# Issuing the head of a gate/up pass inside the stage before it, in a two-layer linear-attention and gated-MLP kernel

## The chip, the cores and the metric

One Trainium2 chip, one of its cores. The metric is the device time of one execution in microseconds (us), the median of several runs. Engines: PE (matmul), DVE (VectorE), ACT (ScalarE), POOL (GpSimd), SP (issues the DMAs).

## The reference

The input x has 2048 tokens of width D = 1024 in bfloat16. Block A and block B are applied twice, with the same weights both times:

```
def _A_ref(x, wqkv, wo):                 # 32 heads of 32
    q, k, v = split(x @ wqkv)
    phi = lambda t: jnp.where(t > 0, t + 1, jnp.exp(t)) + 1e-6
    pq, pk = phi(q), phi(k)
    kv, z = einsum("bhsd,bhse->bhde", pk, v), einsum("bhsd->bhd", pk)
    o = einsum("bhqd,bhde->bhqe", pq, kv) / (einsum("bhqd,bhd->bhq", pq, z)[..., None] + 1e-6)
    return merge_heads(o) @ wo
def _B_ref(x, w_gate, w_up, w_down):     # F = 3584
    return ((x @ w_gate) * (x @ w_up)) @ w_down

x = x + _A_ref(_layernorm(x), wqkv, wo)
x = x + _B_ref(_layernorm(x), w_gate, w_up, w_down)
(the same two lines again)
```

## The kernel before

Every operation goes through one recorder, `P.add(engine, fn, reads, writes)`: an engine runs its operations in the order in which they are recorded, and waits are put in where a region of SBUF, a PSUM bank or a DMA demands one. So the order of the Python calls is the order of each engine's queue, and a waiting instruction holds all that stand behind it on its engine. DMAs are all issued by SP, in recorded order too. An instruction's line in the profile is that of the helper that records it (L662 is any DVE tensor_tensor of the helper `tt`, L665 any scalar_tensor_tensor of `stt`, L404 any plain DMA).

Tokens are handled in 16 tiles of 128. A layer is one `layer_A` and one `layer_B`.

`layer_A`: projections of k and q (L767), then 16 matrix chunks (L851), each with a small product `kvt` (L863) whose last result of each half DVE masks (L868). Beside the chunks `norm(i)` prepares the queries of one tile: DVE multiply (L787), reduce (L790), add (L792), reciprocal (L794), POOL multiply (L796), and a transposing DMA. `NNORM` = 14 of the 16 run there. Then come four held-back q projections, among them `wprod` (L891), matmuls whose results DVE (L898) and ACT (L896) evacuate. Last is the **y loop**, over the 16 tiles: two matmul groups of eight for each tile (`y_grp`, L939), the first added to the residual by DVE (L945), the second seeded (L933) and evacuated (L947) by ACT, in four banks in turn. Beside it the layer norm for block B (class `LN`) goes through a pipeline of one step per tile: statistics on DVE (`start`, L430), a scale (`b1_one`, L441), the normalised row by ACT (`b2_one`, L447) into one of two row buffers `O_XN`, and a transposing DMA from it (`step_t`, L518).

`layer_B`: two passes over 1024 tokens each. A pass is `gateup` (14 pairs of weight columns, Strassen-Winograd products of 512-column matmuls, L1016) and `down` (seven products "1 2 7 4 6 5 3", each four tiles of two groups of seven matmuls, L1285). Weights come through a ring of five slots (`ring_issue`). The order of the steps in a pair is written out by hand in `ORDERS[(second layer, pass)]`: `P` is a product, `D` its last product and `M` the evacuation, `T` a tick that runs other DVE work, `R` a ring load, `S1`/`S5` the weight sums of one pair, and a mark `+` or `'` takes the step of the pair after or before. `L2SETS` names products that are split a second time, into seven groups of two 256-column matmuls (L1082): `11`, `16`, `17` are the steps of product 1, with results handed on in between by ACT (`seed`, L1097; L1107; L1125) and DVE (`join`, L1100). Layer 1 pass 0 splits none and makes its weight combinations itself (`prep_s`); layer 1 pass 1 splits products 1 and 5 and makes the weight sums on DVE; layer 2 splits 1, 5, 3, 2 in both passes and loads the sums (`sp_load`) from what layer 1 stored. The combinations of the activations (`x_ops`, in the list `XQ`) are popped one by one: in the y loop, in products 6 and 5 of `down(0)`, and at the latest where a step needs them (`x_need`).

The first steps of a pass have nothing between them: the pass starts with the steps marked `+` alone, since no other pair is under way.

Of the kernel before, what the change touches and what calls it, by code (L numbers as in the profile page):

```python
# [180 lines left out]
def build_kernel(nc, A_x, A_wqkv, A_wo, B_w_gate, B_w_up, B_w_down, out):  # L181
# [52 lines left out]
    O_ZACC = O_WQ + SZ_W  # L234
    O_GT = O_ZACC + 4096
    RB = take(NST * D * 2)
    O_XR = RB
# [54 lines left out]
    KTA = [dkey("ta%d" % i) for i in range(2)]  # L292
    KTL = [dkey("tl%d" % i) for i in range(2)]
    KTF = [dkey("tf%d" % i) for i in range(NST)]
# [11 lines left out]
    with ExitStack() as es:  # L306
# [62 lines left out]
        B_Z = [5, 6]  # L369
        B_YY = [5, 6, 7, 3]  # L370
        B_GX = [0, 1]
        B_GY = [2, 3]
# [81 lines left out]
        class LN:  # L454
# [12 lines left out]
            def dst(self, n):  # L467
                if self.to == "A0":
                    return xr[:, n, :], r_xr(n)
                return xn[n % 2], R(O_XN[n % 2], D * 2)  # L470

# [42 lines left out]
            def transpose(self, n):  # L514
                d, r = self.dst(n)
                i = self.order[n]
                if self.use_dma:
                    P.add("sp", lambda e: e.dma_start_transpose(xnT[:, :, i * 128:(i + 1) * 128], d),  # L518
                          rd=r, wr=r_xT(i * 128, (i + 1) * 128), dma_sem=KTF[i] if self.to == "A0" else KTL[n % 2])
# [82 lines left out]
        def stash(i):  # L602
            dma(xscr[i * 128:(i + 1) * 128, :], x_res[:, i, :], R(V_X + i * 32, 32), KXS[i], rd=r_x(i))

        def sp_place(ps_, p, g):
            xp = O_X + (8 * ps_ + 3) * D * 2
            o = {"12": (xp, RC), "53": (xp + 4096, O_R + 12288)}[g][p % 2]
            return o, R(V_SP + 64 * p + 32 * SPG.index(g), 32)
# [16 lines left out]
        def sp_load(ps_, p, g):  # L625
            if (first_b[0], ps_, p, g) in sp_done:
                return
            sp_done.add((first_b[0], ps_, p, g))
            o, rv = sp_place(ps_, p, g)
            dma(vh(o, 2048), spscr[2 * p + SPG.index(g)], R(o, 4096), KSP[g, p % 2], rd=rv)  # L630

# [125 lines left out]

        def layer_A(lnp, nxt, first):
            kq_i = [0]
# [141 lines left out]
            for n in range(2 * KT):  # L901
# [24 lines left out]
            for g in range(4, 8):  # L926
                wprod(NG + g, [0, 2, 1, 3][g - 4], g % 2 == 0)
            proj_q(*held[3])()

            def y_seed(n):  # L930
                if n < NST:
                    xs, bank = x_res[:, tok[n], 512:1024], B_YY[(2 * n + 1) % 4]
                    P.add("act", lambda e: e.copy(psb(bank), xs), rd=r_x(tok[n], 512, 1024), pwr=[bank])  # L933

            def y_grp(i, dh, n):
                bank = B_YY[(2 * n + dh) % 4]

# [17 lines left out]
            for i in range(NST):  # L955
                if na[0] < NST:
                    if i % 3 == 2:
                        norm(tok[na[0]])
                        na[0] += 1
                elif RG["n"] < NR:  # L960
                    ring_issue()
                nxt.step_t(1)
                nxt.b1_one()
                if i >= 2 and (first or i < 14):
                    nxt.start(i - 2)
                y_grp(tok[i], 0, i)
                y_seed(i + 1)
                nxt.b2_one()
                y_grp(tok[i], 1, i)
                if not first and i == 12:  # L970
                    for k in range(5):
                        stash(3 + k)
                if not first and i == 14:
                    first_b[0] = False
                    for g in SPG:
                        sp_load(0, 0, g)
                if nxt.t_next >= 8 and not RG["tq"]:
                    RG["tq"] = True
                    XQ.extend(x_ops(0, L2SETS[not first, 0]))
                x_pop(2 if i > 11 else 1)  # L980
            nxt.use_dma = False
            nxt.on_act = False

        def layer_B(lnp, nxt, first):
            is_last = nxt is None
            lnp.use_dma = True
            lnp.on_act = False
            lnp.need(7)
            if not RG["tq"]:
                XQ.extend(x_ops(0, L2SETS[not first, 0]))  # L990
            if not is_last:
                nxt.use_dma = True
                nxt.on_act = False

            def pair(ps_, p, l2):
# [159 lines left out]
                def sums(g, mode):  # L1155
# [17 lines left out]
                    tt(sp[:, 3], wA[:, :, 1], sp[:, 1], ALU.subtract, rp[1] + rA, rp[3])  # L1173
                    dma(spscr[2 * p + SPG.index(g)], vh(o, 2048), rv, KSPW[g, p % 2], rd=R(o, 4096))

# [13 lines left out]
            def gateup(ps_, ticks, l2):  # L1189
# [7 lines left out]
                def emit(it, tk):  # L1197
# [10 lines left out]
                    if p == 0:  # L1208
                        x_need(tk)
                        x_pop()  # L1210
                    if tk[0] == "P":
# [19 lines left out]

                if jit:
                    prep_s(n0)
                    prep_s(n0 + 1)
                for it in range(-1, NP):
                    for tk in order:
                        emit(it, tk)

                def tail():
# [9 lines left out]
                return tail  # L1249

            def down(ps_, ticks, tail):
                i0 = ps_ * 8
# [18 lines left out]
                for qi, q in enumerate(DPROD):  # L1271
# [75 lines left out]
            def dticks0(q, t):  # L1347
# [39 lines left out]

            if first:
                wd_tick(0)
            if first:  # L1390
                for k in range(5):
                    stash(3 + k)
            tail = gateup(0, ticks0, L2SETS[not first, 0])
            if first:
                wd_tick(2 * NJ)
            lnp.need(NST - 1)
            XQ.extend(x_ops(1, L2SETS[not first, 1]))
            down(0, dticks0, tail)
            tail = gateup(1, ticks1, L2SETS[not first, 1])
            down(1, dticks1, tail)  # L1400
            lnp.use_dma = False
            lnp.on_act = False
        dh0 = D // 2
# [16 lines left out]
        alt = [4, 5, 6, 7, 0, 1, 2, 3, 12, 13, 14, 15, 8, 9, 10, 11]  # L1420
        lnA = LN("A0", nat)
        lnB = LN("B", nat)
        layer_A(lnA, lnB, True)
        lnA = LN("A", alt)
        layer_B(lnB, lnA, True)
        lnB = LN("B", alt)
        layer_A(lnA, lnB, False)
        layer_B(lnB, None, False)

# [37 lines left out]
```

## Time and profile before

| | us |
|---|---|
| median of 3 runs | 1486.23 |
| lowest, highest | 1483.78, 1487.76 |
| the profiled execution, its own time | 1487.03 |
| its span, first to last instruction | 1485.3 |
| PE busy | 1459.4 |
| DVE busy | 1089.3 |
| ACT busy | 572.7 |
| POOL busy | 216.1 |
| mean granted PE clock | 0.999 |

All times below are from the start of the span. A busy matmul is longer than the step from one to the next, since they are pipelined: the time lost before a late group is counted from where the group would have started.

### The profile page before, as it was taken

How to read it: one execution, taken by the hardware profiler on the slowest of the kernel's cores; microseconds unless marked ns; L12 is line 12 of the kernel's file. 1: busy time of each engine (PE TensorE's matmuls, PEld its weight loads, DVE VectorE, ACT ScalarE, POOL GpSimd, SP SyncE). 2: the span in 40 equal slices, each digit the busy share in tenths (PEclk: the TensorE clock that was granted, in tenths of full speed). 3: DMA queues.
4: the chain of work that ended last, by engine and by line, in shares of the span. 5: the costliest groups of instructions: out<-in, count | busy, mean ns of one | idle time of the engine just before them, and what ended most of it. 6: DMA issues, size and time to landing. Idle time of an engine off the chain costs nothing.

```text
span 1485.3 us, 20620 instructions
## 1 busy us (share of the span) xinstructions
PE 1459.4 (98%) x7830; PEld 749.3 (50%) x7830; DVE 1089.3 (73%) x1990; ACT 572.7 (39%) x1179; POOL 216.1 (15%) x239
## 2 busy tenths in 40 slices
PE   8999989999999999999999999999999999999999
PEld 3434434444444455554444444446666445666544
DVE  7976777877766599875569769879877575777753
ACT  3332246333310155550013322477776004777400
POOL 4542632000000000000024337210000000000000
PEclk9999999999999999999999999999999999999999
DMA  8799746988885789975364437677965766777642
GB/s 269 131 171 235 160 120 156 272 262 262 261 286 184 231 260 293 295 261 204 124 213 109 132 94 149 178 180 253 283 265 199 237 210 227 261 265 253 210 172 97
DMA packets 268338, 312.78 MB, mean 211 GB/s; under 512 B 161616, under 2 KB 214608, under 8 KB 268240
## 3 DMA queue, kind: packets, MB, share of 16 engines
q1 hardware_dynamic: 268240, 311.48, 69.5%
q8 instruction: 61, 1.00, 0.3%
q14 instruction: 37, 0.30, 0.1%
HBM read 233.31 MB, written 69.21 MB: 204 GB/s over the span
## 4 chain that ended last, share of the span: by engine, by line
PE 88%; DMA 5%; DVE 5%; issue 1%; ACT 1%; POOL 1%; SPq 0%; DVEq 0%; ACTq 0%; POOLq 0%
PE ps L1016 29%; PE ps L1285 23%; PE ps L1082 14%; PE ps L767 12%; PE ps L851 5%; DMA arena<-arena 4%; PE ps L939 4%; DVE arena L787 1%; DVE arena L790 1%; DVE arena L430 1%; DMA arena<-in_A_wqkv_dram 1%; DMA arena<-sp_scratch 1%; DVE arena L662 0%; POOL arena L796 0%; PE ps L891 0%
## 5 line engine op out<-in xcount | busy, mean ns | idle before, releaser
L665 DVE SCALAR_TENSOR_TENSOR arena<-ps,arena 128x512 f16<-128x512 f32 (+2 forms) x508 | 340.5, 686 | 204.0 <-PE ps L1285 150.4
L1016 PE MATMUL ps<-arena 128*128 128x512 f16 x2016 | 478.7, 379 | 1.0 <-DVE arena L662 1.0
L662 DVE TENSOR_TENSOR arena<-arena 128x512 f16<-128x512 f16 (+4 forms) x624 | 309.3, 520 | 60.3 <-ACT arena L1125 48.8
L1285 PE MATMUL ps<-arena 128*128 128x512 f16 (+1 forms) x1568 | 339.4, 379 | 0.0
L1016 PEld LDWEIGHTS ps<-arena 128*128 128x128 f16 (+1 forms) x2016 | 192.1, 98 | 188.3 <-ACT arena L1021 13.6
L1082 PE MATMUL ps<-arena 128*128 128x256 f16 x1960 | 259.4, 273 | 6.6 <-DVE ps L1100 2.4
L1285 PEld LDWEIGHTS ps<-arena 128*128 128x128 f16 x1568 | 153.4, 98 | 185.0
L1082 PEld LDWEIGHTS ps<-arena 128*128 128x128 f16 (+1 forms) x1960 | 189.1, 98 | 90.7 <-DVE ps L1100 11.1
L767 PE MATMUL ps<-arena 128*128 128x512 bf16 x1024 | 225.4, 380 | 8.0 <-DMA arena<-arena 4.6
L1021 ACT ACTIVATE arena<-ps 128x512 f16<-128x512 f32 x224 | 133.7, 597 | 114.9 <-PE ps L1016 113.0
L576 ACT ACTIVATE arena<-ps 128x512 f32<-128x512 f32 x128 | 76.3, 597 | 243.7 <-PE ps L767 221.7
L767 PEld LDWEIGHTS ps<-arena 128*128 128x128 f16 x1024 | 99.3, 98 | 129.3 <-DMA arena<-arena 8.2
L1097 ACT COPY ps<-ps 128x256 f32<-128x256 f32 x168 | 61.8, 369 | 212.5 <-PE ps L1082 210.0
L851 PE MATMUL ps<-arena 128*128 128x512 bf16 x512 | 115.4, 379 | 0.0
L433 POOL TENSOR_SCALAR arena<-arena 128x1 f32<-128x1 f32 x64 | 21.0, 327 | 629.5 <-DVE arena L432 629.5
L939 PE MATMUL ps<-arena 128*128 128x512 bf16 x512 | 111.0, 379 | 1.1 <-ACT ps L933 1.1
L1046 ACT COPY ps<-ps 128x512 f32<-128x512 f32 x112 | 64.2, 573 | 87.7 <-PE ps L1016 52.1
L430 DVE BATCH_NORM_STATS2 arena<-arena 128x6 f32<-128x512 bf16 x128 | 88.1, 688 | 10.7 <-DMA arena<-in_A_x_dram 6.2
L796 POOL TENSOR_TENSOR arena<-arena 128x1024 f16<-128x1024 f32 x32 | 78.2, 2444 | 97.9 <-DVE arena L794 81.1
L577 DVE TENSOR_SCALAR arena<-arena 128x512 f32<-128x512 f32 x128 | 65.8, 514 | 35.6 <-ACT arena L576 34.5
L579 DVE SCALAR_TENSOR_TENSOR arena<-ps,arena 128x512 bf16<-128x512 f32 x128 | 88.5, 691 | 4.4
L1100 DVE TENSOR_TENSOR ps<-ps,arena 128x256 f32<-128x256 f32 x168 | 69.3, 427 | 27.3 <-PE ps L1082 13.7
(51 smaller groups left out, 712.7 us busy)
## 6 DMA issues: line engine op xcount, KB each, us to landing
arena<-w_scratch SPq DMA_DIRECT2D x84, 896.0 KB, 5.5
arena<-t_scratch SPq DMA_DIRECT2D x32, 896.0 KB, 5.5
arena<-sp_scratch SPq DMA_DIRECT2D x56, 512.0 KB, 5.2
arena<-in_B_w_down_dram SPq DMA_DIRECT2D x24, 896.0 KB, 5.8
w_scratch<-arena SPq DMA_DIRECT2D x28, 512.0 KB, 7.5
sp_scratch<-arena SPq DMA_DIRECT2D x28, 512.0 KB, 3.7
arena<-in_A_wqkv_dram SPq DMA_DIRECT2D x12, 1024.0 KB, 9.1
arena<-w_scratch SPq DMA_DIRECT2D x28, 384.0 KB, 6.0
```

Of the source, the lines that this page charges most:

```text
L430: P.add("dve", (lambda h: lambda e: e.bn_stats(st[j][:, 6 * h:6 * h + 6], x_res[:, i, (D // 2) * h:(D // 2) * (h + 1)]))(h), rd=r_x(i, (D ...
L579: P.add("dve", lambda e: e.scalar_tensor_tensor(out=dst_ap, in0=psb(bank), scalar=0.0, in1=etmp[r], op0=ALU.max, op1=ALU.add), prd=[bank], ...
L662: P.add("dve", lambda e: e.tensor_tensor(out=out, in0=a, in1=b, op=op), rd=rd, wr=wr, prd=prd)
L665: P.add("dve", lambda e: e.scalar_tensor_tensor(out=out, in0=a, scalar=sc, in1=b, op0=ALU.mult, op1=op1), rd=rd, wr=wr, prd=prd)
L767: return [e.matmul(psb(bank), xnT[:, k, i * 128:(i + 1) * 128], w[:, k, h * 512:(h + 1) * 512], start=(k == 0), stop=(k == KT - 1)) for k ...
L796: P.add("pool", lambda e: e.tensor_tensor(out=asb[b].rearrange("p (h c) -> p h c", c=32), in0=pbuf.rearrange("p (h c) -> p h c", c=32), in ...
L851: return [e.matmul(psb(bank), xr[:, t, j * 128:(j + 1) * 128], pk[:, h, t, :], start=(t == 0), stop=(t == NST - 1)) for t in range(NST)]
L939: return [e.matmul(psb(bank), xnT[:, g, i * 128:(i + 1) * 128], wp[:, g, dh * 512:(dh + 1) * 512], start=(dh == 0 and g == 0), stop=(g == ...
L1016: P.add("pe", lambda e: [e.matmul(psb(bank), w[:, k, :], x[:, k, :], start=(start and k == 0), stop=(k == 3), skip_group_check=True) for k ...
L1021: P.add("act", lambda e: e.activation(t, psb(bank), AF.Copy, scale=SG), prd=[bank], wr=r)
L1082: P.add("pe", lambda e: [e.matmul(psb(bank)[:, 256 * half:256 * half + 256], w[:, k, :], xx[:, k, :], start=(start and k == 0), stop=(k == ...
L1285: return [e.matmul(psb(bank), hv[:, 7 * hf + k, t * 128:(t + 1) * 128], w[:, k, :], start=(start and hf == 0 and k == 0), stop=(hf == 1 an ...
```

## The change

1. **Heads.** `gateup` is cut in two. The steps from its beginning up to the first one that is not in the list `early` form a list `pro`; `pro_step(pro, 1)` takes steps off it until one has issued matmuls. In `down(0)`, product 3, one such step follows each group of seven for tiles 1 to 3 (six places); in the y loop one stands between the two groups of the last tile. What is left of `pro` runs at the head of the pass. Layer 1 pass 0 has no `pro`.
2. **Row buffers.** Rows 0 to 9 of `LN("B")` use four buffers instead of two (the two new ones lie in the space of the q weights).
3. **Norm.** In layer 1 the 14th `norm` moves from the last chunk to behind the last held q projection, ahead of the y loop.
4. **Y loop.** `start` runs a tile earlier; ring loads 4 and 5 are issued at tiles 12 and 13; `XQ` is popped by a budget from tile 11 on; layer 1 does `prep_s` at tiles 13 and 14; layer 2 puts tiles 8 to 15 into banks 0 to 3.
5. **Sums.** `sp_load` of the first pairs uses the other buffer first, in layer 2 pass 0; the stashing of five tiles of x moves behind the y loop; the sums "12" of pair 1 are loaded ahead of the pass; two `XQ` steps instead of one are popped per tile in product 6.
6. **Order** of layer 2 pass 0 rewritten.

```
-  (True, 0): "D2A T1 26 37 T0+ 35 P6A 27 51 P6B 25 S1+ S5+ M2A 11+ 56 P7A D2B F3 M2B Ra 57 Rb P5A 16+ P7B P5B M5A M5B D4A 17+ M4A D3A M3A D3B P1A+ M3B 31+ 21+ D4B 36+ M4B P1B+",
+  (True, 0): "D2A 26 T1 T0+ 37 P6A 35 27 25 M2A 51 S1+ P6B 11+ 56 F3 D2B M2B P7A 57 P5A M5A P7B 16+ Ra S5+ P5B D4A Rb M5B 17+ D3A M4A D3B P1A+ M3A M3B 31+ 21+ D4B 36+ M4B P1B+",
...
+    O_XN += [O_WQ, O_WQ + D * 2]
...
+  def buf(self, n):
+      return n % 4 if self.to == "B" and n < 10 else n % 2
...
+  def sp_buf(ps_, p):
+      return (p + 1 - ps_) % 2
...
+  def x_budget(w):
+      while XQ and w > 0:
+          w -= 3 if XQ[0][0][0] == "t" else 1
+          x_pop()
...
-      if n >= 2 and na[0] < NNORM:
+      if n >= 2 and na[0] < NNORM - first:
           norm(tok[na[0]])
...
   proj_q(*held[3])()
+  if na[0] < NNORM:
+      norm(tok[na[0]])
+      na[0] += 1
...
-      elif RG["n"] < NR:
+      elif i > 11 and RG["n"] < NR:
           ring_issue()
       nxt.step_t(1)
-      nxt.b1_one()
-      if i >= 2 and (first or i < 14):
-          nxt.start(i - 2)
       y_grp(tok[i], 0, i)
+      if i < NST - 1:
+          nxt.b1_one()
+      if i and (first or i < 12):
+          nxt.start(i - 1)
       y_seed(i + 1)
-      nxt.b2_one()
+      if i < NST - 1:
+          nxt.b2_one()
+      if i == NST - 1:
+          pro_step(pro, 1)
       y_grp(tok[i], 1, i)
       if not first and i == 12:
-          for k in range(5):
-              stash(3 + k)
-      if not first and i == 14:
           first_b[0] = False
           for g in SPG:
               sp_load(0, 0, g)
...
-      x_pop(2 if i > 11 else 1)
+      if i > 10:
+          x_budget(5)
+      if first and i in (13, 14):
+          prep_s(i - 13)
...
+  def pro_step(pro, n):
+      for _ in range(n):
+          k = len(P.streams["pe"])
+          while pro and len(P.streams["pe"]) == k:
+              pro.pop(0)()
...
+  seq = [(it, tk) for it in range(-1, NP) for tk in order if tk[0] == "R" or 0 <= it + {"'": -1, "+": 1}.get(tk[-1], 0) < NP]
+  early = ("11", "16", "17", "P1", "21", "26", "27", "31", "36", "37", "S1", "S5", "T0", "T1", "Ra", "Rb")
+  npro = 0 if jit else [tk[:2] in early for _, tk in seq].index(False)
+  pro = [(lambda x=x: emit(*x)) for x in seq[:npro]]
...
               if qi == 0 and t == 0 and hf == 0:
                   tail()
+              if q == "3" and t:
+                  pro_step(pro, 1)
...
           for g in SPG:
               sp_load(1, 0, g)
+          sp_load(1, 1, "12")
       if q in "65":
-          x_pop(1 if q == "6" else 3)
+          x_pop(2 if q == "6" else 3)
```

More of the change, by code (lines that the diff above doesn't have):

```diff
@@ L292, in build_kernel @@
     KTA = [dkey("ta%d" % i) for i in range(2)]
-    KTL = [dkey("tl%d" % i) for i in range(2)]
+    KTL = [dkey("tl%d" % i) for i in range(4)]
     KTF = [dkey("tf%d" % i) for i in range(NST)]
@@ L370, in build_kernel @@
         B_YY = [5, 6, 7, 3]
+        B_YE = [0, 1, 2, 3]
         B_GX = [0, 1]
@@ L469, in dst @@
                     return xr[:, n, :], r_xr(n)
-                return xn[n % 2], R(O_XN[n % 2], D * 2)
+                b = self.buf(n)
+                return xn[b], R(O_XN[b], D * 2)
+            def buf(self, n):
+                return n % 4 if self.to == "B" and n < 10 else n % 2
             def start(self, i):
@@ L518, in transpose @@
                     P.add("sp", lambda e: e.dma_start_transpose(xnT[:, :, i * 128:(i + 1) * 128], d),
-                          rd=r, wr=r_xT(i * 128, (i + 1) * 128), dma_sem=KTF[i] if self.to == "A0" else KTL[n % 2])
+                          rd=r, wr=r_xT(i * 128, (i + 1) * 128), dma_sem=KTF[i] if self.to == "A0" else KTL[self.buf(n)])
                     return
@@ L629, in sp_load @@
             o, rv = sp_place(ps_, p, g)
-            dma(vh(o, 2048), spscr[2 * p + SPG.index(g)], R(o, 4096), KSP[g, p % 2], rd=rv)
+            dma(vh(o, 2048), spscr[2 * p + SPG.index(g)], R(o, 4096), KSP[g, sp_buf(ps_, p)], rd=rv)
         def unit_jm(u):
@@ L756, in wd_store, with layer_A @@
             dma(tscr[:, :, j, :].rearrange("q p c -> p q c"), dout, R(V_D + j * 32, 32), KDW, rd=R(O_DOUT, 4096))
-        def layer_A(lnp, nxt, first):
+        def layer_A(lnp, nxt, first, pro):
             kq_i = [0]
@@ L928, in layer_A, with y_bank @@
             proj_q(*held[3])()
+            if na[0] < NNORM:
+                norm(tok[na[0]])
+                na[0] += 1
+            def y_bank(n, dh):
+                return (B_YY if n < 8 or first else B_YE)[(2 * n + dh) % 4]
             def y_seed(n):
                 if n < NST:
-                    xs, bank = x_res[:, tok[n], 512:1024], B_YY[(2 * n + 1) % 4]
+                    xs, bank = x_res[:, tok[n], 512:1024], y_bank(n, 1)
                     P.add("act", lambda e: e.copy(psb(bank), xs), rd=r_x(tok[n], 512, 1024), pwr=[bank])
             def y_grp(i, dh, n):
-                bank = B_YY[(2 * n + dh) % 4]
+                bank = y_bank(n, dh)
                 def fn(e):
@@ L1173, in sums @@
                     tt(sp[:, 3], wA[:, :, 1], sp[:, 1], ALU.subtract, rp[1] + rA, rp[3])
-                    dma(spscr[2 * p + SPG.index(g)], vh(o, 2048), rv, KSPW[g, p % 2], rd=R(o, 4096))
+                    dma(spscr[2 * p + SPG.index(g)], vh(o, 2048), rv, KSPW[g, sp_buf(ps_, p)], rd=R(o, 4096))
                 def fin(q, c):
@@ L1209, in emit @@
                         x_need(tk)
-                        x_pop()
+                        if tk[0] in "PDM":
+                            x_pop()
                     if tk[0] == "P":
@@ L1230, in emit @@
                         c["L"][tk[0]]["st" + tk[1]]()
[L1232 to L1237, printed above, removed]
+                seq = [(it, tk) for it in range(-1, NP) for tk in order
+                       if tk[0] == "R" or 0 <= it + {"'": -1, "+": 1}.get(tk[-1], 0) < NP]
+                early = ("11", "16", "17", "P1", "21", "26", "27", "31", "36", "37", "S1", "S5", "T0", "T1", "Ra", "Rb")
+                npro = 0 if jit else [tk[:2] in early for _, tk in seq].index(False)
+                pro = [(lambda x=x: emit(*x)) for x in seq[:npro]]
                 def tail():
@@ L1248, in tail, with run, down @@
                         dma(x_res[:, i, :], xscr[i * 128:(i + 1) * 128, :], r_x(i), KX[i], rd=R(V_X + i * 32, 32))
-                return tail
-            def down(ps_, ticks, tail):
+                def run():
+                    pro_step(pro, len(pro))
+                    for x in seq[npro:]:
+                        emit(*x)
+                    return tail
+                return pro, run
+            def down(ps_, ticks, tail, pro=()):
                 i0 = ps_ * 8
@@ L1386, in dticks1, with run @@
                             stash(8 + k)
-            if first:
-                wd_tick(0)
-            if first:
+            pro0, run0 = gateup(0, ticks0, L2SETS[not first, 0])
+            pro1, run1 = gateup(1, ticks1, L2SETS[not first, 1])
+            def run():
+                lnp.use_dma = True
+                lnp.on_act = False
+                lnp.need(7)
+                if not RG["tq"]:
+                    XQ.extend(x_ops(0, L2SETS[not first, 0]))
+                if not is_last:
+                    nxt.use_dma = True
+                    nxt.on_act = False
                 for k in range(5):
                     stash(3 + k)
[L1393 to L1402, printed above, removed]
+                if first:
+                    wd_tick(0)
+                else:
+                    sp_load(0, 1, "12")
+                tail = run0()
+                if first:
+                    wd_tick(2 * NJ)
+                lnp.need(NST - 1)
+                XQ.extend(x_ops(1, L2SETS[not first, 1]))
+                down(0, dticks0, tail, pro1)
+                down(1, dticks1, run1())
+                lnp.use_dma = False
+                lnp.on_act = False
+            return pro0, run
         dh0 = D // 2
@@ L1420, in build_kernel @@
         alt = [4, 5, 6, 7, 0, 1, 2, 3, 12, 13, 14, 15, 8, 9, 10, 11]
[L1421 to L1428, printed above, removed]
+        lnA, lnA2 = LN("A0", nat), LN("A", alt)
+        lnB, lnB2 = LN("B", nat), LN("B", alt)
+        pro, run_b = layer_B(lnB, lnA2, True)
+        layer_A(lnA, lnB, True, pro)
+        run_b()
+        pro, run_b = layer_B(lnB2, None, False)
+        layer_A(lnA2, lnB2, False, pro)
+        run_b()
         P.plan({KOUT} | set(KPK))
```

10 lines of the change are left out of this document (1 added, 9 removed).

## The prediction

> **What bounds the kernel now.** I read the busy times first, then busy time by stage, then PE's own rows around each seam between stages.
>
> ```profile
> PE 1459.4 (98%) x7830; PEld 749.3 (50%) x7830; DVE 1089.3 (73%) x1990; ACT 572.7 (39%) x1179; POOL 216.1 (15%) x239
> ```
>
> PE is the bound, so only time in which PE stands can be won. The stages come next: span, then busy time of PE, weight load, DVE, ACT and POOL, then the granted clock.
>
> ```profile
> 183.30:198.34 15.04, 10.59 (x49) 4.33 (x47) 12.50 (x20) 4.57 (x8) 7.44 (x3) 0.89 0.71 160
> ...
> 198.34:253.59 55.25, 55.25 (x257) 24.97 (x256) 43.09 (x83) 32.65 (x45) 14.01 (x28) 1.00 0.51 113
> 933.27:989.82 56.55, 55.42 (x257) 24.96 (x256) 42.99 (x85) 32.42 (x44) 13.22 (x26) 1.00 0.74 193
> ...
> 508.58:669.71 161.13, 158.96 (x927) 90.24 (x926) 136.24 (x305) 90.19 (x193) 6.96 (x16) 1.00 0.91 282
> 989.82:1151.52 161.70, 159.46 (x1121) 107.87 (x1120) 132.21 (x263) 116.24 (x295) 3.96 (x8) 1.00 0.70 240
> 1236.13:1397.66 161.53, 159.35 (x1122) 108.85 (x1120) 121.66 (x241) 115.62 (x294) 0.00 (x0) 1.00 0.70 245
> ```
>
> These are layer 1's attention tail, the two y loops, and the gate/up passes of layer 1 pass 1 and of layer 2 (pass 0, pass 1). PE stands 4.45 us in the tail, at a clock of 0.89, 1.13 in the second y loop, and about 2.2 in each pass. The layer 1 y loop has no gap. How fast PE goes when nothing is late, from the chain of waits (start, us, what):
>
> ```profile
> 1249.75 2.18 PE ps L1082 x20
> ...
> 1397.82 84.62 PE ps L1285 x392
> ```
>
> So a 512-column matmul steps in 0.216 us (84.62 / 392) and a 256-column one in 0.109. Below, "idle" in brackets begins only when the last matmul has drained: a pair of 256-column matmuls shows as 0.39 us but steps in 0.22, so each wait loses its idle time plus 0.17.
>
> **The attention tail of layer 1 (norm moved).** PE, then DVE, then the same place in layer 2:
>
> ```profile
> 185.05 0.39 PE L863 MATMUL ps<-arena 128*128 128x128 bf16 x4
> 185.27 1.89 PE L767 MATMUL ps<-arena 128*128 128x512 bf16 x8
> 190.69 1.89 PE L891 MATMUL ps<-arena 128*128 128x512 bf16 x4 [3.53 <-DVE arena L868]
> 192.37 2.45 PE L767 MATMUL ps<-arena 128*128 128x512 bf16 x8
> 194.66 0.81 PE L891 MATMUL ps<-arena 128*128 128x512 bf16 x3
> 196.38 0.39 PE L891 MATMUL ps<-arena 128*128 128x512 bf16 x1 [0.92 <-DVE arena L898]
> ```
>
> ```profile
> 186.44 0.35 DVE L794 RECIPROCAL arena<-arena 128x32 f32<-128x32 f32 x1
> 186.71 1.16 DVE L787 TENSOR_TENSOR arena<-arena 128x1024 f32<-128x1024 bf16 x1
> ...
> 190.01 0.63 DVE L868 TENSOR_TENSOR arena<-ps,arena 128x512 bf16<-128x512 f32 x1
> ...
> 926.01 0.39 PE L863 MATMUL ps<-arena 128*128 128x128 bf16 x4
> 926.43 0.69 DVE L868 TENSOR_TENSOR arena<-ps,arena 128x512 bf16<-128x512 f32 x1 [1.57 <-PE ps L863]
> ```
>
> The mask multiply L868 stands on DVE behind the 14th norm, which holds it from 186.71 to 190.01. In layer 2 it starts 0.42 after the matmuls. From L863 to the y loop layer 1 takes 198.34 - 185.05 = 13.29, layer 2 takes 933.27 - 926.01 = 7.26: 6.03 us are lost. This includes four matmuls that took 1.68 us (190.69 to 192.37) instead of 0.86. With the norm gone from there, L868 starts at 186.71 instead of 190.01. That is 1.66 after L863's start, 1.24 later than in layer 2. There PE had the eight matmuls (1.73) to spare from 926.23, and L868's result 0.69 later at about 927.1, so 0.86 of the lateness is covered and PE waits some 0.4. The later evacuations on the same DVE may pass on up to another 0.86. Gain 6.03 - 0.4 = 5.6 down to 4.8; I take 5.2. Slow matmuls are counted in it, since no wait of over 1 us is left.
>
> The Trainium skill ("TensorE: Matmul & The Clock Gate", Part 1) says that PE's clock halves after an idle window of about 3.4 us and comes back after as long at work. The trace agrees: 3.53 idle, then clock 0.89. By that figure the slow stretch would cost 3.4 / 2 = 1.7 us, where the rows give 1.4 (0.82 and 0.56 on the next eight), and the sum below would be 0.3 larger; it is an estimate.
>
> The norm itself, 3.30 us of DVE (186.71 to 190.01), now stands ahead of the first addition of the y loop. That addition began 1.93 after the loop did:
>
> ```profile
> 200.27 0.69 DVE L945 TENSOR_TENSOR arena<-ps,arena 128x512 bf16<-128x512 f32 x1
> ```
>
> With the norm it ends at 1.93 + 3.30 + 0.69 = 5.9; its bank is wanted by tile 2, at 2 x 3.45 = 6.9 (16 matmuls a tile). So it is hidden by 1.0 us. DVE works 43.09 of 55.25 there and catches up. If the cover fails, up to 3.3 come back.
>
> **Row buffers in the second y loop.**
>
> ```profile
> 964.98 1.24 ACT L447 ACTIVATE arena<-arena 128x1024 f16<-128x1024 bf16 x1 [2.79 <-DMA arena<-arena]
> ...
> 967.37 0.82 PE L939 MATMUL ps<-arena 128*128 128x512 bf16 x3 [1.13 <-ACT ps L933]
> ```
>
> ACT waits for the transposing DMA to free a row buffer, so the seed behind it on ACT is late, and PE stands 1.13. Twice the buffers, and ring loads moved from beside these transposes to tiles 12 and 13, end that: 1.13 + 0.17 = 1.3 (also 56.55 - 55.25). Bounds 0 and 1.3; I take 1.3.
>
> **The four heads.** Only the rows that begin with a wait:
>
> ```profile
> 255.61 0.60 PE L1016 MATMUL ps<-arena 128*128 128x512 f16 x2 [1.00 <-DVE arena L662]
> ...
> 509.86 0.39 PE L1082 MATMUL ps<-arena 128*128 128x256 f16 x2 [0.90 <-DVE arena L662]
> 510.99 0.39 PE L1082 MATMUL ps<-arena 128*128 128x256 f16 x2 [0.74 <-ACT arena L1107]
> 511.91 1.26 PE L1082 MATMUL ps<-arena 128*128 128x256 f16 x10 [0.53 <-DVE ps L1100]
> ...
> 991.24 0.39 PE L1082 MATMUL ps<-arena 128*128 128x256 f16 x2 [0.81 <-ACT arena L1107]
> 992.78 1.92 PE L1082 MATMUL ps<-arena 128*128 128x256 f16 x14 [1.15 <-DVE ps L1100]
> 994.85 0.39 PE L1082 MATMUL ps<-arena 128*128 128x256 f16 x2 [0.15 <-ACT arena L1125]
> ...
> 1237.47 0.39 PE L1082 MATMUL ps<-arena 128*128 128x256 f16 x2 [0.74 <-ACT arena L1107]
> 1238.54 1.92 PE L1082 MATMUL ps<-arena 128*128 128x256 f16 x14 [0.69 <-DVE ps L1100]
> 1240.61 0.61 PE L1082 MATMUL ps<-arena 128*128 128x256 f16 x4 [0.15 <-ACT arena L1125]
> ...
> 1245.24 0.83 PE L1082 MATMUL ps<-arena 128*128 128x256 f16 x6 [0.54 <-DMA arena<-sp_scratch]
> ```
>
> At a head PE does steps 11, 16, 17 with nothing in between, and each waits for ACT or DVE to hand on.
>
> *Layer 1 pass 0* (255.61): loses 1.17 on the weight combinations. They now stand at tiles 13 and 14, where DVE has more than it can do for a moment (two `XQ` steps and a combination a tile) but is done before the matmul that reads them. Gain 1.1; 0.6 if DVE is late.
>
> *Layer 1 pass 1*: loses 0.90 + 0.74 + 0.53 + 3 x 0.17 = 2.7. All four `pro` steps now lie between groups of 7 x 0.216 = 1.51, longer than each link (509.86 to 510.99 is 1.13, of which 0.22 is its own work). But step 11 reads a sum that needs the second weight slot:
>
> ```profile
> 484.60 12.41 SPq L404 DMA_DIRECT2D arena<-w_scratch  x3
> ...
> arena<-w_scratch SPq DMA_DIRECT2D x5, 896.0 KB, 6.3
> ```
>
> Product 3 starts 12.1 (56 x 0.216) before 508.58, at 496.5. The second of those three loads can go when product 5's last first half ends, 1.51 earlier, at 495.0, and lands 6.3 later (median), at 501.3. The step stands behind three groups of 1.51, at 501.0, and needs one sum more (0.5). So it may hold `down` for about 0.8. I take a gain of 1.9; 1.0 to 2.7.
>
> *Layer 2 pass 0*: loses 0.81 + 1.15 + 0.15 + 3 x 0.17 = 2.6. Only step 11 moves, between the two groups of the last tile; 16 and 17 stay back to back, and DVE is busy there:
>
> ```profile
> 988.30 0.69 DVE L945 TENSOR_TENSOR arena<-ps,arena 128x512 bf16<-128x512 f32 x1 [0.49 <-PE ps L939]
> 988.90 3.47 DVE L662 TENSOR_TENSOR arena<-arena 128x512 f16<-128x512 f16 x7
> ```
>
> Seven such steps take 0.50 each; the new budget leaves five (2.5) behind the last addition, about as long as PE's second group. So 11 to 16 is won (1.0) and some 0.3 given back. Gain 0.7; 0 to 1.8.
>
> *Layer 2 pass 1*: loses 0.74 + 0.69 + 0.15 + 0.54 + 4 x 0.17 = 2.8. Six steps move into `down`; their weights and sums are loaded a product ahead, and the sums of pair 1, late at 1245.24, go out with them. Left is step 26 waiting for the copies of 21 (0.3). Gain 2.5; 1.5 to 2.8.
>
> **Order of layer 2 pass 0, and the rest.** The two layer 2 passes differ by 161.70 - 161.53 = 0.17 with heads of about the same loss, so a pair is already at the pace of its matmuls and the new order can win at most about 0.3; I take 0.2. Below, it can lose (first rival); 2.0 if one idle of 0.15 as at 1240.61 comes in each of 13 pairs. The stash, moved behind the y loop, stands on SP ahead of the sums of pair 1 only; two steps per tile in product 6 add DVE work where PE doesn't wait for it. Both at nothing; uncovered, the sums cost what they do at 1245.24, 0.7.
>
> **Sum.** 5.2 + 1.3 + 1.1 + 1.9 + 0.7 + 2.5 + 0.2 = 12.9. The profiled execution took 1487.0 (0.8 above the median), so 1474.1.
>
> **Rivals.**
> 1. *Slower: the new order waits in every pair.* Between `16+` and `17+` the old order had three 512-column groups (2.6 us), the new two (1.73). The link took 992.78 - 991.24 = 1.54 with DVE busy, 1.07 at 1237.47 to 1238.54. If DVE, busy 132.21 of 161.70 here, comes late by 0.2 to 0.7, PE waits. From 1.0 a pair (12.9 / 13) the gain is gone; with the whole link bare it is 13 x 1.54 = 20, so 1494. Against it: pass 1 keeps DVE nearly as busy (121.66) without a wait. 6%.
> 2. *The heads hold the row they were put in.* PE keeps the order of its matmuls, so a step that is late holds the groups of `down` or y behind it. Then heads give about a third of 5.1: 1477.5. The Trainium skill ("TensorE: Matmul & The Clock Gate", Part 2) says that only weight loads are pulled ahead and matmuls stay in program order. No row of this trace tells against it. 15%.
> 3. *The y loops pay.* DVE (norm, combinations, `XQ`) falls behind by more than the 1.0 us of cover and PE waits 3 to 5: 1478. 11%.
> 4. *The change moves waits only*: tail, heads and order give less than 4.4 net, about 1484. 7%.
>
> **How the numbers follow.** The forecast's own range takes the upper gains (5.6 + 1.3 + 1.2 + 2.7 + 1.8 + 2.8 + 0.3 = 15.7: 1471.3) and half the lower ones (1478), 61%. With rivals 2 and 3 it reaches 1481; below, the runs of before spread 2.5 under their median, so 1469.5. A measurement can tell about 0.3% (4.5 us) from no change: faster 0.87 (forecast, 2 and 3), same 0.07 (rival 4), slower 0.06.
>
> **What would show it.** L868 some 1.7 after L863 in layer 1 and no matmul of 0.43 us behind it; tail near 7.7; second y loop at 55.3; no wait on L447 that reaches PE; in product 3 of `down` L1082 rows between L1285 rows, without idle before either; passes that begin with 512-column matmuls or step 51. Wrong would be: idle at L1285 in product 3, idle at L939 in tiles 2 to 7 of layer 1, or layer 2 pass 0 longer than 161.7.

## The result and the profile after

| | before | after |
|---|---|---|
| median, us | 1485.51 (1483.78 to 1487.76, 4 runs) | 1469.90 (1469.07 to 1470.04, 4 runs) |
| ratio, 95% interval | | 0.9893 [0.9876, 0.9910] |
| profiled execution, its span | 1487.03, 1485.3 | 1470.04, 1468.3 |

Before has one run more than above. 15.6 us less, where 13 were forecast. The matmul lines move with the change: L767 is now L781, L851 L865, L891 L905, L939 L959, L1016 L1038, L1082 L1104, L1285 L1313.

Busy time by stage in the profile after (span; busy PE, weight load, DVE, ACT, POOL; clock; DMA). The stages are the attention tail of layer 1, the y loops of layer 1 and 2 (the second with step 11 in it), and what is left of the gate/up passes of layer 1 pass 1, layer 2 pass 0 and pass 1:

```profile
180.30:191.72 11.42, 9.24 (x48) 4.01 (x46) 11.12 (x17) 4.69 (x8) 4.96 (x3) 1.00 0.62 133
191.72:246.98 55.26, 55.26 (x258) 25.05 (x257) 48.51 (x94) 33.14 (x45) 21.49 (x29) 1.00 0.62 134
922.61:978.30 55.69, 55.69 (x262) 25.44 (x260) 44.45 (x87) 31.57 (x45) 15.16 (x24) 1.00 0.72 192
502.11:659.06 156.95, 156.95 (x916) 89.39 (x915) 132.57 (x295) 88.82 (x189) 6.99 (x16) 1.00 0.92 282
978.30:1137.56 159.26, 158.51 (x1117) 108.69 (x1116) 130.19 (x261) 115.73 (x293) 5.00 (x10) 1.00 0.73 245
1223.91:1380.70 156.79, 156.77 (x1106) 107.70 (x1104) 119.51 (x235) 113.59 (x288) 0.00 (x0) 1.00 0.70 248
```

The passes lose at most 0.75 us of PE where they lost 2.2, the second y loop nothing where it lost 1.13, and the granted clock is 1.00 in each of these rows. PE's rows at the four heads, in order of time:

```profile
246.98 15.27 PE L1038 MATMUL ps<-arena 128*128 128x512 f16 x70
...
493.24 0.60 PE L1104 MATMUL ps<-arena 128*128 128x256 f16 x4
493.68 1.67 PE L1313 MATMUL ps<-arena 128*128 128x512 bf16 x7
495.19 0.38 PE L1104 MATMUL ps<-arena 128*128 128x256 f16 x2
495.41 1.67 PE L1313 MATMUL ps<-arena 128*128 128x512 bf16 x7
...
976.13 0.60 PE L1104 MATMUL ps<-arena 128*128 128x256 f16 x4
976.57 1.89 PE L959 MATMUL ps<-arena 128*128 128x512 bf16 x8
978.30 0.38 PE L1104 MATMUL ps<-arena 128*128 128x256 f16 x2
979.22 3.55 PE L1104 MATMUL ps<-arena 128*128 128x256 f16 x26 [0.54 <-DVE ps L1122]
...
1221.97 0.60 PE L1104 MATMUL ps<-arena 128*128 128x256 f16 x4
1222.40 1.67 PE L1313 MATMUL ps<-arena 128*128 128x512 bf16 x7
1223.91 2.02 PE L1104 MATMUL ps<-arena 128*128 128x256 f16 x16
```

Head steps stand between groups of `down` (L1313) and of the last y tile (L959), without idle before either. One wait is left: step 17 for step 16 in layer 2 pass 0.

In the tail, PE and then DVE:

```profile
182.06 0.39 PE L877 MATMUL ps<-arena 128*128 128x128 bf16 x4
182.29 1.89 PE L781 MATMUL ps<-arena 128*128 128x512 bf16 x8
184.94 1.04 PE L905 MATMUL ps<-arena 128*128 128x512 bf16 x4 [0.76 <-DVE arena L882]
185.81 1.89 PE L781 MATMUL ps<-arena 128*128 128x512 bf16 x8
187.54 0.81 PE L905 MATMUL ps<-arena 128*128 128x512 bf16 x3
189.77 0.39 PE L905 MATMUL ps<-arena 128*128 128x512 bf16 x1 [1.42 <-DVE arena L912]
190.00 1.89 PE L781 MATMUL ps<-arena 128*128 128x512 bf16 x8
```

```profile
184.25 0.63 DVE L882 TENSOR_TENSOR arena<-ps,arena 128x512 bf16<-128x512 f32 x1
184.80 1.81 DVE L583 TENSOR_SCALAR arena<-arena 128x512 f32<-128x512 f32 x1
```

The mask multiply comes 2.19 after L877's start (4.96 before), and no matmul is slow. But PE still waits twice, and a small DVE step (L583, part of the evacuation of a q projection) takes 1.81.

Stage by stage, from one matmul anchor to the next, the two profiles differ so:

| stretch | before | after | gain | forecast |
|---|---|---|---|---|
| start to the first chunk | 122.36 | 119.01 | 3.35 | 0 |
| chunks | 62.69 | 63.05 | -0.36 | 0 |
| tail of layer 1 | 13.29 | 9.66 | 3.63 | 5.2 |
| y loop of layer 1 | 55.25 | 55.26 | 0 | 0 |
| layer 1 pass 0 | 169.52 | 168.34 | 1.18 | 1.1 |
| first `down` and pass 1 of layer 1 | 246.60 | 243.74 | 2.86 | 1.9 |
| y loop and pass 0 of layer 2 | 218.25 | 214.95 | 3.30 | 1.3 + 0.7 + 0.2 |
| first `down` and pass 1 of layer 2 | 246.14 | 243.14 | 3.00 | 2.5 |

All the rest agrees to 0.05. The stretches that the change touches give 14.0. The 3.35 lies ahead of them, in the first projections.

### The profile page after: what moved, and what is told of

Same layout as the page of the kernel before. It is cut to its first block, busy times and chain, and to the rows that moved or that the text cites. A ratio compares the mean times of both kernels' runs of the same rounds, so it can differ in the third digit from the quotient of the medians.

```text
span 1468.3 us, 20619 instructions
## 1 busy us (share of the span) xinstructions
PE 1455.5 (99%) x7830; PEld 751.8 (51%) x7830; DVE 1089.8 (74%) x1990; ACT 572.1 (39%) x1178; POOL 224.0 (15%) x239
## 4 chain that ended last, share of the span: by engine, by line
PE 94%; DVE 3%; DMA 2%; SPq 0%; ACT 0%; issue 0%; POOL 0%; DVEq 0%; POOLq 0%
PE ps L1038 30%; PE ps L1313 23%; PE ps L1104 15%; PE ps L781 13%; PE ps L959 7%; PE ps L865 5%; DMA arena<-arena 2%; DVE arena L801 1%; DVE arena L804 1%; DMA arena<-in_A_wqkv_dram 1%; SPq L406 0%; PE ps L877 0%; DVE arena L806 0%; PE ps L905 0%; DVE arena L808 0%; DVE arena L583 0%
## 5 line engine op out<-in xcount | busy, mean ns | idle before, releaser
L1038 PE MATMUL ps<-arena 128*128 128x512 f16 x2016 | 478.6, 379 | 0.0
L1313 PE MATMUL ps<-arena 128*128 128x512 f16 (+1 forms) x1568 | 340.9, 379 | 0.0
L1038 PEld LDWEIGHTS ps<-arena 128*128 128x128 f16 (+1 forms) x2016 | 192.3, 98 | 186.7 <-ACT arena L1043 13.6
L1104 PE MATMUL ps<-arena 128*128 128x256 f16 x1960 | 259.4, 273 | 0.8 <-DVE ps L1122 0.5
L1313 PEld LDWEIGHTS ps<-arena 128*128 128x128 f16 x1568 | 153.4, 98 | 183.1
L1104 PEld LDWEIGHTS ps<-arena 128*128 128x128 f16 (+1 forms) x1960 | 190.9, 98 | 83.3 <-DVE ps L1122 3.8
L781 PE MATMUL ps<-arena 128*128 128x512 bf16 x1024 | 224.2, 379 | 5.1 <-DMA arena<-arena 2.4
L582 ACT ACTIVATE arena<-ps 128x512 f32<-128x512 f32 x128 | 76.3, 597 | 236.1 <-PE ps L781 221.9
L781 PEld LDWEIGHTS ps<-arena 128*128 128x128 f16 x1024 | 99.4, 98 | 124.7 <-DMA arena<-arena 3.9
L435 POOL TENSOR_SCALAR arena<-arena 128x1 f32<-128x1 f32 x64 | 27.2, 425 | 642.9 <-DVE arena L434 642.9
L865 PE MATMUL ps<-arena 128*128 128x512 bf16 x512 | 115.4, 379 | 0.0
L959 PE MATMUL ps<-arena 128*128 128x512 bf16 x512 | 111.0, 379 | 0.0
L1122 DVE TENSOR_TENSOR ps<-ps,arena 128x256 f32<-128x256 f32 x168 | 70.7, 428 | 33.5 <-PE ps L1104 16.6
L583 DVE TENSOR_SCALAR arena<-arena 128x512 f32<-128x512 f32 x128 | 67.2, 525 | 30.3 <-ACT arena L582 29.3
L810 POOL TENSOR_TENSOR arena<-arena 128x1024 f16<-128x1024 f32 x32 | 77.4, 2417 | 77.4 <-DVE arena L808 65.1
```

The lines of the kernel that those rows point to most:

```text
L781: return [e.matmul(psb(bank), xnT[:, k, i * 128:(i + 1) * 128], w[:, k, h * 512:(h + 1) * 512], start=(k == 0), stop=(k == KT - 1)) for k ...
L810: P.add("pool", lambda e: e.tensor_tensor(out=asb[b].rearrange("p (h c) -> p h c", c=32), in0=pbuf.rearrange("p (h c) -> p h c", c=32), in ...
L865: return [e.matmul(psb(bank), xr[:, t, j * 128:(j + 1) * 128], pk[:, h, t, :], start=(t == 0), stop=(t == NST - 1)) for t in range(NST)]
L959: return [e.matmul(psb(bank), xnT[:, g, i * 128:(i + 1) * 128], wp[:, g, dh * 512:(dh + 1) * 512], start=(dh == 0 and g == 0), stop=(g == ...
L1038: P.add("pe", lambda e: [e.matmul(psb(bank), w[:, k, :], x[:, k, :], start=(start and k == 0), stop=(k == 3), skip_group_check=True) for k ...
L1104: P.add("pe", lambda e: [e.matmul(psb(bank)[:, 256 * half:256 * half + 256], w[:, k, :], xx[:, k, :], start=(start and k == 0), stop=(k == ...
```

## The experiments

**The same kernels again, for what varies by itself.**

> The changed kernel once more, on the chip of the next three. Of the 17.0 us by which its first profile is shorter, 3.35 lie ahead of the first chunk matmul (L851 before at 122.36, L865 after at 119.01), where the change did nothing. Theory: that is the spread of the DMA waits in the first projections, so the chunks begin anywhere from 119 to 122.5 here and the stages the change touches repeat to 0.1 us (tail 9.66 from L877 to the y loop). Rival: the change brings it in some way; then they begin at 119.0 again, and in every kernel below.

> The kernel before, profiled once more. In its first profile the chunks began at 122.36 and the tail took 13.29; in the eight undisturbed profiles of changed kernels that have run the chunks began at 117.4 to 120.5, and with one norm moved the tail took 7.26 to 9.66. Theory: both vary from one execution to the next, by how late the transposing DMAs leave DVE's norms, so here the chunks begin at 117 to 121 and the tail takes 10.5 to 13.3. Rival: the kernel before is late there by itself; 122 and 13.3 again.

The changed kernel took 1468.24 (0.989 [0.987, 0.9909]). Its chunks began at 119.48 and its tail took 7.26, not 9.66: the "repeats to 0.1 us" of the expectation was wrong for the tail. The kernel before, again, took 1484.34: chunks at 121.11, tail 11.80. And its first y loop, without a gap in the first profile, now had one; the tail's longest wait is shown ahead of it, and no matmul behind that wait is slow:

```profile
187.94 1.04 PE L891 MATMUL ps<-arena 128*128 128x512 bf16 x4 [2.03 <-DVE arena L868]
...
229.38 1.90 PE L939 MATMUL ps<-arena 128*128 128x512 bf16 x8 [0.82 <-ACT ps L933]
```

Over the 13 profiles other than that of norm_dve (below), the chunks begin anywhere from 117.42 to 122.36 (118.12 to 122.36 in three profiles with the old stages, 117.42 to 120.54 in ten with the new), and the tail with one norm moved takes 7.26 to 9.66. The chunks themselves take 62.68 to 64.05. Later stretches of the same code repeat within 0.5, but for the y loops with two row buffers and the old pass 0 of layer 1 (168.61 to 169.52).

Ahead of the chunks PE waits 5.85 us for DMAs in the first profile before and 3.10 in the first after. So most of the 3.35 us is the spread of these waits; a smaller shift by the change itself is not ruled out, since two of the three old profiles begin later than all ten new ones. The second pair of profiles, before_again and after_again, differs by 16.6 us: 1.6 in the start and 15.0 in the stretches that the change touches.

**The norm, put back, taken twice, and moved alone.**

```
 norm_back:  if n >= 2 and na[0] < NNORM:              (in the changed kernel)
 norm_two:   if n >= 2 and na[0] < NNORM - 2 * first:  (in the changed kernel)
 norm_only:  if n >= 2 and na[0] < NNORM - first:      (in the kernel before,
             with the norm behind the last held projection)
```

> The changed kernel with the 14th norm of layer 1 back among the chunks. Theory: DVE holds the mask multiply (L882) for one norm more, PE stands about 3.5 us and the clock falls again; tail 13.3 as before, 3.6 longer than with the move, time about 3.6 above the changed kernel. Rival: the gain in the tail came from elsewhere (ring loads, sums); then the tail stays under 11 and the time moves by less than 1.5.

> The changed kernel with two norms of layer 1 taken from among the chunks: the 13th goes behind the last held q projection, the other three to tiles 2, 5 and 8 of the y loop. In the changed kernel the tail still loses 9.66 - 7.26 = 2.4 us. Theory: it is the DVE and POOL work of the 13th norm, so the tail falls to 7.3 to 7.8 and the time by 1.9 to 2.4. Rival: the y loop has no room for one more norm and PE waits in it; then the y loop grows over 55.3 by what the tail wins.

> The kernel before with the norm moved alone. Theory: the tail takes 7.3 to 9.7 and all else stays as before, time 3 to 4 under the kernel before. Rival: without the later ring loads and the four row buffers the first y loop is disturbed by the norm (its DMA transposes and row reload), and it grows by 1 or more over 55.25.

Put back: 1471.80 (1471.07 to 1473.55), 3.6 above the changed kernel on the same chip (1467.71 to 1469.17), as the theory said. The tail in its profile was 10.54: less than the 13.3 expected, without a slow matmul, and under the 11 that was the rival's sign. The rest of the rival fails: against after_again its tail is 3.28 longer and its span 3.3, and all other stretches agree to 0.05. PE's waits in that tail:

```profile
185.03 1.04 PE L905 MATMUL ps<-arena 128*128 128x512 bf16 x4 [0.77 <-DVE arena L882]
...
188.23 0.97 PE L905 MATMUL ps<-arena 128*128 128x512 bf16 x3 [0.44 <-ACT arena L910]
190.73 0.39 PE L905 MATMUL ps<-arena 128*128 128x512 bf16 x1 [1.53 <-DVE arena L912]
```

The last two go back to POOL. The 14th norm's row (`O_P[1]`) lies in the space that ACT's L582 writes (`O_E`), so L582 stood until the norm's POOL multiply ended, at 186.42, and L583 stood 2.17 for L582. In the changed kernel the last norm among the chunks is the 13th, whose row lies elsewhere.

Taken twice: 1467.27 (1466.74 to 1470.18), 1.0 below the changed kernel where 1.9 to 2.4 were expected; the executions of the two overlap, so by time no gain is shown. The tail took 7.26, which the changed kernel reaches by itself in after_again. The y loop is still 55.25, so the rival (no room in it) falls. PE's rows in the tail have no wait left:

```profile
184.59 0.39 PE L877 MATMUL ps<-arena 128*128 128x128 bf16 x4
184.81 1.89 PE L781 MATMUL ps<-arena 128*128 128x512 bf16 x8
186.54 1.03 PE L905 MATMUL ps<-arena 128*128 128x512 bf16 x4
187.40 1.89 PE L781 MATMUL ps<-arena 128*128 128x512 bf16 x8
189.13 1.16 PE L905 MATMUL ps<-arena 128*128 128x512 bf16 x4
190.12 1.89 PE L781 MATMUL ps<-arena 128*128 128x512 bf16 x8
```

Moved alone, in the kernel before: the tail fell to 7.26, but the time only to 1479.15, 0.998 [0.9969, 0.9991] of the kernel before on that chip, 2.8 us where 3 to 4 were expected. The first y loop grew to 57.03. ACT waited there for a row buffer, as in layer 2:

```profile
215.68 1.24 ACT L447 ACTIVATE arena<-arena 128x1024 f16<-128x1024 bf16 x1 [4.19 <-DMA arena<-arena]
...
220.26 1.24 ACT L447 ACTIVATE arena<-arena 128x1024 f16<-128x1024 bf16 x1 [2.25 <-DMA arena<-arena]
```

The rival's place is right here. Whether the moved norm or chance (0.82 idle above, without it) makes it 1.8 is not settled. In the changed kernel the four buffers take it away.

**The POOL multiply beside the tail.**

```
+  if not late:                         # late: the 13th norm of layer 1
+      norm_fin(i, "pool")
...
   proj_q(*held[3])()
+  if first:
+      norm_fin(tok[NNORM - 2], "dve")
```

> The changed kernel, where the last multiply of the 13th norm in layer 1 (POOL, L810) is done by DVE behind the last held q projection; all its DVE work stays in place. In the changed kernel one DVE step beside that POOL multiply took 1.81 us (L583 at 184.80) where it takes 0.43 elsewhere. Theory: the POOL multiply slows that DVE step, and with it the wait of 1.42 at L905; without it L583 takes 0.43, that wait falls under 0.4, the tail to about 8.3. Rival: L583 is long for what stands before it on DVE; then it and the tail stay (9.4 to 9.7).

Three executions took 1466.27 to 1466.64, 1.6 below the changed kernel on that chip. The fourth, the profiled one, took 6766 (last section), so the tail can't be read. The time fits the theory, but since the changed kernel's own tail varies by 2.4 it doesn't tell the two causes apart. The other profiles do. In the changed kernel's first profile L583 takes 0.37 to 0.43 us in 99 of 128 cases and 0.57 to 1.81 in 29. In each of the 29 a POOL operation on a tile of 128x512 or more had begun before it and was still running, and in 28 of them L583 ends 0.27 to 0.29 after that operation (in the other the view joins two POOL operations). Here it is 184.80 + 1.81 against POOL's 184.42 + 1.91; then in after_again, DVE ahead of POOL:

```profile
183.21 0.72 DVE L583 TENSOR_SCALAR arena<-arena 128x512 f32<-128x512 f32 x1
...
181.73 1.91 POOL L810 TENSOR_TENSOR arena<-arena 128x1024 f16<-128x1024 f32 x1 [0.53 <-DVE arena L808]
```

So the theory's first link holds: the POOL multiply lengthens L583. With two norms moved, L583 comes behind that multiply and takes 0.42. That the tail falls to 8.3 without it is not shown. The Trainium skill ("SBUF — State Buffer", Who interferes with whom) says that a DVE tensor_scalar in its fast mode and a POOL instruction lock a port pair against each other, and that the later one stands until the first is done. These rows agree.

**Row buffers and ring loads.**

```
 rows_two:   return n % 2                               (two row buffers)
 ring_early: elif RG["n"] < NR:                         (ring loads as before)
 rows_ring:  both
```

> The changed kernel with two row buffers again, the ring loads still at tiles 12 and 13. Theory (the buffers ended the wait of ACT on the transposing DMA): waits on L449 come back and PE stands about 1 us in the second y loop, 56.2 to 56.7 without the head step in it. Rival (the moved ring loads ended it): no wait that reaches PE, y loop 55.25.

> The changed kernel with four row buffers and the ring loads back at the first free tiles. Theory (the buffers did it): y loop of layer 2 stays at 55.25, PE does not wait. Rival (ring loads): the wait is back, about 56.5.

> Both undone: two row buffers and early ring loads. By either theory the wait of about 1.1 us in the second y loop is back (56.2 to 56.7). If it is not, the earlier start of the layer norm, by one tile, ended it.

Each of the three ran once, so they are read by stretches (times 1468.08, 1469.13 and 1471.56). From the y loop's start to the first 512-column matmul of layer 2 pass 0 the changed kernel takes 60.00, and so does ring_early (60.01). With two buffers (rows_two) it takes 61.02, with both undone 62.91. The layer 1 y loops are, in the order ring_early, rows_two, rows_ring, 55.25, 56.62 and 57.22. So the buffers ended the wait, in both layers, and not the earlier start of the layer norm; the later ring loads do nothing with four buffers. With two, the execution with late loads waited less, but with one execution each that is not shown to be their doing. The 2.9 us of rows_ring in layer 2 is about twice what was expected (1.0 to 1.5); why is open. Row and wait of rows_two, layer 1, then the longest wait of rows_ring in layer 2:

```profile
215.70 1.24 ACT L449 ACTIVATE arena<-arena 128x1024 f16<-128x1024 bf16 x1 [3.79 <-DMA arena<-arena]
```

```profile
218.08 2.12 PE L959 MATMUL ps<-arena 128*128 128x512 bf16 x8 [1.20 <-ACT ps L953]
```

```profile
956.92 3.41 PE L959 MATMUL ps<-arena 128*128 128x512 bf16 x15 [1.89 <-ACT ps L953]
```

**No heads.**

```
-  npro = 0 if jit else [tk[:2] in early for _, tk in seq].index(False)
+  npro = 0
```

> The changed kernel with no step of a pass issued ahead of it: every list of head steps is empty, all else as changed. Theory: the heads of layer 1 pass 1 and of both layer 2 passes wait again, 2.7 + 1.0 + 2.1 (without the wait on sums, which are still loaded early) = 5.8 us, about 1475.7. Rival: the earlier sums and steps of the activations did part of it, so the heads alone are worth 3 or less, 1473.

The three stretches grew by 2.87 (first `down` and pass 1 of layer 1), 0.97 (second y loop to the first 512-column matmul) and 2.05 (layer 2 pass 1): 5.9, all of it at the heads. The time was 1474.41, 0.9931 [0.9907, 0.9956] of the kernel before on that chip. The theory holds. Layer 1 pass 1 waits as in the kernel before:

```profile
500.60 0.39 PE L1104 MATMUL ps<-arena 128*128 128x256 f16 x2 [0.90 <-DVE arena L671]
501.74 0.39 PE L1104 MATMUL ps<-arena 128*128 128x256 f16 x2 [0.74 <-ACT arena L1129]
502.65 1.27 PE L1104 MATMUL ps<-arena 128*128 128x256 f16 x10 [0.53 <-DVE ps L1122]
```

In pass 1 of layer 2, 0.95 of its 3.0 stays won without heads: that is the early load of sums (0.54 + 0.17 in the forecast's terms) and 0.2 of other waits. In pass 0 of layer 2 about 0.6 of the head's 1.6 stays won too: the wait before step 17, 1.15 in the kernel before, is 0.53 here. That the new budget of `XQ` steps did this is likely, but no run takes it apart.

**The old order.** This run was meant to be the changed kernel with the old line of `ORDERS` for layer 2 pass 0.

> The changed kernel with the old order of layer 2 pass 0. Theory: a pair takes 11.315 us instead of 11.293, 0.3 in all, and the head keeps its waits, since the head steps come in the same order; about 0.3 longer from the y loop to down. Rival: the new order carries the gain at this head (2.0 measured, 0.9 predicted); then 1 or more longer.

The kernel that ran is the changed kernel letter for letter, with the new line. So neither the theory nor the rival is tested, and no run shows what the order gives. It is one more execution of the changed kernel: 1469.10, tail 9.10, head and pass the same as in its other two (60.00, 154.95). From its first 512-column matmul the pass takes 154.95 with the new order, and 155.35 in the kernel before; a pair takes 11.29 and 11.32. No wait of PE shows in the pairs of either. Whether the 0.4 us come from the order or from another part of the change is open.

**A version meant to beat both.** Two norms moved, and one more head step ahead of the last tile:

```
+  if i == NST - 1:
+      pro_step(pro, 1)
   y_grp(tok[i], 0, i)
```

> A version meant to beat both: the changed kernel with two norms of layer 1 moved out of the chunks, and in the y loops' last tile one head step more, ahead of its first group (so steps 11 and 16 of layer 2 pass 0 both lie before the pass). Expected: tail 7.26 in every execution, the wait of 0.54 between steps 16 and 17 gone, 1 to 2.5 us under the changed kernel. Rival: step 17's hand-over is only moved on to step 21, and the y loop has no room for the norm; no gain.

1466.72 (1465.33 to 1467.18), 0.9887 [0.987, 0.9903] of the kernel before on that chip. The tail took 7.26 in the one profile; y loop to first 512-column matmul 59.41 instead of 60.00. So the rival is half right, a wait of 0.33 has moved on:

```profile
975.74 1.25 PE L1106 MATMUL ps<-arena 128*128 128x256 f16 x10
977.33 2.08 PE L1106 MATMUL ps<-arena 128*128 128x256 f16 x16 [0.33 <-DVE ps L1124]
```

By the stretches it wins 0.6 and up to 2.4 (the tail); its ratio to the kernel before and the changed kernel's overlap, so by time alone it isn't shown to be faster than the changed kernel.

## Why the prediction was right, and where it was off

The direction was right, and so were the places and mechanisms of the tail, the row buffers and the heads: the waits of each came back when its part was undone. The gain of the order is not shown. The range held the time near its lower end. Off were sizes, and that the sum came as near as it did (12.9 forecast, 14.0 in the stretches touched) is partly luck: in the first pair of profiles the tail gave 1.6 less than forecast and the heads 2.4 more.

*Tail: 5.2 forecast, 3.6 measured (profile pair, and norm_back by time).* The term that failed is the lateness of DVE: L868 was put 1.66 behind L863 and came 2.19 behind in the first profile (0.43 in after_again), and the "another 0.86" that DVE might pass on was 1.42, since the POOL multiply of the norm that stays held L583 for 1.81. One profile was also taken for the kernel: the tail before was 13.29 and 11.80, with the norm put back 10.54; after, 7.26, 9.10 and 9.66 with the very same code. So the gain is 2.1 to 6.0 by the profiles taken, and 5.2 lies within. The slow matmuls came in the first of these tails only: after 3.53 us of idle, not after 2.03. The Trainium skill's window of about 3.4 us ("TensorE: Matmul & The Clock Gate", Part 1) agrees with both.

*Row buffers: 1.3 forecast, 1.3 measured in layer 2.* With two buffers put back it lost 1.0 and, with early ring loads, 2.9. The premise that layer 1's y loop has no gap failed: 0, 1.0 and 1.8 over 55.25 in three executions of the old stage, 55.25 in all with four buffers. The norm of 3.3 us ahead of that loop stayed hidden in each of those with four.

*Heads: 1.1, 1.9, 0.7 and 2.5 forecast; 1.18, 2.86, about 1.6 and 3.0 measured.* The 1.18 of layer 1 pass 0 is that of the first pair. In before_again that pass takes 168.61, only 0.26 more than after, and no wait stands at its head: the y loop ahead of it had lost 1.0 instead. The two stretches together take 224.77 and 224.86 before, 223.60 after, so about 1.2 is won in both pairs, once at the head and once mostly in the y loop. In layer 1 pass 1 the wait of 0.8 for the second weight slot did not come: the load was issued at 487.39 and the sums began at 492.74, so it landed within 5.3, not at the median of 6.3, and the sum is wanted by the step's third matmul, not its first. This is rival 2's mechanism; no head holds a group in any row. In layer 2 pass 0 the steps behind 17 were expected to wait as before, and 26 matmuls ran on from 979.22: DVE had its five `XQ` steps done by 978.8 (forecast: about the end of PE's second group, 978.3) and the hand-over at 979.2, so only one wait of 0.54 is left. By no_heads, the heads themselves are worth 1.0 of the 1.6 here, and 5.9 in all in layer 1 pass 1 and layer 2. In pass 1 of layer 2 the 0.3 at step 26 did not come, since PE's groups covered it.

*Order: 0.2 forecast; at most 0.4 measured in the pass, and not told apart from the rest of the change.* Rival 1, a wait in each pair, did not come (11.29 a pair with the new order, 11.32 in the kernel before). Rivals 3 and 4 fall with the y loops at 55.25 and the stretches at 14.0.

*The rest.* 14.0 of 17.0 in the profile pair; the other 3.0 lies ahead of the tail, for the most part in the spread of the start, which the forecast counted as nothing and left to its range. In the second pair it was 15.0 of 16.6.

## What to carry to other kernels

Short chains of hand-overs at the head of a PE-bound stage cost what their links take, and can go between the matmul groups of the stage before, if their operands and banks are free there: 2.9 us at one head here. Before a stall is priced from one profile, see whether it repeats: the tail's varied by 2.4 us with the same code, and a stage with no gap lost 1.0 the next time. And a gain won in one stage can be missing in the sum: with the norm moved alone the tail fell to 7.26, but the y loop behind it lost 1.8 for want of row buffers, by the norm or by chance.

## What the runs showed of the hardware

A DVE step of 0.43 us (L583) took 1.81 beside a POOL multiply that began first, and 0.57 or more in all 29 cases of one profile in which a POOL operation on a tile was already running. The other way round, POOL's multiply (L810) takes 1.91 at its shortest and 2.77 in the changed kernel at 181.12, where a norm's DVE multiply (L801) began 0.16 before it. In one execution, of norm_dve, the matmuls of every stage were slow, at a recorded mean clock of 1.000: those of 512 columns took 1256 to 1409 ns in the mean of their lines, where the kernel before has 379, and the span was 6764.4 us. Its three other executions took 1466. The costliest line, with its busy us and mean ns:

```profile
L1045 PE MATMUL ps<-arena 128*128 128x512 f16 x2016 | 2217.7, 1393 | 0.0
```

What caused it is open; no other execution on record shows it.
